# Transposing the weights piece by piece inside the forward chain, and storing them in on-chip layout, in a recurrent attention + SwiGLU training step

## The chip, the cores and the metric

One core of a Trainium2 chip. The metric is the device time of one execution in microseconds (us), lower is better. Before the prediction three executions of the kernel before were known: 3452.7 us median (3452.23 to 3463.88). A difference counts as faster or slower when it is over 2%. DRAM below is the device memory outside the core, SBUF the on-chip memory.

## The reference, cut to what matters

A forward pass and all its gradients. A sequence of 2048 tokens of width 448 goes through layer norm and an attention with memory in 64 *serial* segments: each takes 8 memory rows from the one before it. A SwiGLU feed-forward network (FFN) follows. The outputs are the result and nine gradients.

```python
# S=2048, D=448, H=16, Dh=256, M=8, seg=32 -> 64 segments;  FFN width F=1792; all bf16
for s in range(n_seg):
    h = concat([mem, x[s*32:(s+1)*32]])          # 40 rows
    q, k, v = h @ Wq, h @ Wk, h @ Wv             # 448 x 4096 each
    o = softmax(mask(q @ k.T * scale)) @ v
    o = o @ Wo                                   # 4096 x 448
    mem = o[:8]; outs.append(o[8:])
...
h  = x + attention(layernorm(x), mem0, Wq, Wk, Wv, Wo)
h2 = h + (silu(n @ w_gate) * (n @ w_up)) @ w_down,  n = layernorm(h)
out, vjp = jax.vjp(f, x, mem0, Wq, Wk, Wv, Wo, w_gate, w_up, w_down)
return (out, *vjp(grad_out))
```

## The kernel before

There are four stages, one after the other: the forward chain (64 segments), the FFN with its backward pass (8 groups of 2 tiles of 128 tokens), the backward chain (64 segments in reverse), and the weight gradients ("last stage"). The forward chain uses the weights as they lie. The FFN's backward pass and the backward chain need them *transposed*, and the kernel makes these transposes by DMA at the moment when a stage starts.

`W`, `A` and `B` are three large SBUF arenas; the numbers are offsets in KB per partition. In the profile `arW`, `arA` and `arB` are these arenas, so "arA<-arA" is a transpose inside SBUF.

```python
def transposed_rows(k, dst, src2d, tmp):                # removed by the change
    for kc in range(3):
        nc.sync.dma_start_transpose(out=dst[:, kc, :], in_=src2d[:, kc * P:(kc + 1) * P])
    nc.sync.dma_start_transpose(out=tmp, in_=src2d[:, k.D - P:k.D])
    nc.sync.dma_start(out=dst[0:64, 3, :], in_=tmp[64:P, :])
...
# forward chain, once per tile (4 segments): turn a block in SBUF, then store it
    def to_token_major(blk, t):
        for hf in range(2):
            ot = stg()                                  # one of two 8 KB staging buffers
            nc.sync.dma_start_transpose(out=ot..., in_=blk[:, 16 * hf:16 * hf + 16, :]...)
            nc.gpsimd.dma_start(out=dr["X_o"][t][:, hf * 2048:(hf + 1) * 2048], in_=ot)
...
# FFN: 48 transposes of 448 KB for the last stage (z, u, g of 16 tiles)
    def tmajor(src, t, tt, dst):
        stg = tstg_b[rot[0] % 3]
        nc.sync.dma_start_transpose(out=stg, in_=src[:, tt]...)
        nc.gpsimd.dma_start(out=dst[t * P:(t + 1) * P, :], in_=stg...)

    for gi in range(NT // G):
        for tt in range(G):
            nc.sync.dma_start(out=h_t, in_=dr["Hh"][rows, :])
            nc.vector.tensor_scalar(out=hn_t[:, 0:D], in0=h_t, ...)           # layer norm
            nc.sync.dma_start_transpose(out=hnT[...], in_=hn_t)
            nc.sync.dma_start(out=dout_t[:, 0:D], in_=GO2[rows, :])
            nc.sync.dma_start_transpose(out=doT[...], in_=dout_t)
        if gi == 0:
            transposed_rows(k, WdT_sb, Wd2, wdT_tmp)                          # w_down^T
            nc.gpsimd.dma_start(out=Wd_sb, in_=Wd2...)
            nc.sync.dma_start_transpose(out=WgT_sb, in_=Wg2)                  # w_gate^T
            nc.sync.dma_start_transpose(out=WuT_sb, in_=Wu2)                  # w_up^T
        ...
            dh_t = k.f32("f3", D, "dh_t")                                     # one buffer
            ln_bwd(k, [(dh_t[:], ...)], ...)
            nc.gpsimd.dma_start(out=dr["DH"][rows, :], in_=dh_t[:])
...
# backward chain, before its first segment
    transposed_rows(k, WoT_sb, k.Wo2, woT_tmp)
    prep_tile(NT - 1)
    load_seg(NSEG - 1)          # transposing loads of VG, QT, KT; plain load of P_all
    for (Wsrc, WT) in ((k.Wk2, WkT_sb), (k.Wv2, WvT_sb), (k.Wq2, WqT_sb)):
        nc.sync.dma_start_transpose(out=WT, in_=Wsrc)
...
# last stage: 96 transposing loads of 512 KB (X_v, X_k, X_q), and packed loads of M_v, M_k, M_q
            nc.sync.dma_start_transpose(out=x_t.rearrange(...), in_=dr["X_" + nm][t][:, ...])
            nc.gpsimd.dma_start(out=ld, in_=dr["M_" + nm][...]...)
```

## Time and profile before

| stage (from, to; us) | length | DMA share | granted TensorE clock |
|---|---|---|---|
| forward chain, 150 to 1160 (inside it) | 1010 | 0.44 | 0.99 |
| forward's last matmul (1181.3) to the start of the second backward segment's softmax gradient (1659.4) | 478.1 | 0.93 | 0.83 |
| backward chain, 1660 to 2730 (inside it) | 1070 | 0.79 | 0.98 |
| last stage, 2734.5 to 3461.7 | 727.2 | 0.72 | 0.98 |

The second row, "between the chains", holds the whole FFN and both of its borders. Its lines and the others come from the busy table by stretches of the kernel before. The columns are: stretch, its length, then busy time (and number of instructions) of TensorE, of TensorE's weight load, of VectorE, ScalarE and GpSimd, the granted clock, the mean busy share of the 16 DMA engines, and GB/s. The DMA share adds up the time that packets took. It can pass 1, and it does not measure bytes.

```profile
150.00:1160.00 1010.00, 950.83 (x23283) 736.94 (x23281) 428.97 (x978) 319.23 (x700) 151.75 (x351) 0.99 0.44 140
1181.30:1659.40 478.10, 312.87 (x2565) 220.53 (x2564) 240.77 (x373) 117.32 (x208) 79.13 (x147) 0.83 0.93 196
2734.50:3461.70 727.20, 682.80 (x3928) 316.70 (x3930) 88.15 (x157) 96.09 (x148) 124.21 (x216) 0.98 0.72 184
```

TensorE is busy 94% of the forward chain and of the last stage, and 65% of the stretch between the chains (312.87 of 478.1). The next lines are TensorE's timeline in that stretch (start, length, engine and line, output<-inputs, count; in brackets the idle time just before and what ended it).

```profile
1243.36 13.43 PE L536 MATMUL psf<-arA,arW 128*128 128x256 bf16 x96 [62.03 <-DMA arA<-arA]
1610.84 4.60 PE L713 MATMUL psf<-arA,arW 128*128 128x40 bf16 x128 [44.81 <-POOL arA L648]
1643.58 7.11 PE L756 MATMUL po<-arW,arA 128*32 128x448 bf16 x96 [19.58 <-DMA arW<-in_A_Wv_dram]
```

There are three holes: 62 us between the forward chain and the first FFN matmul, 45 and 20 us around the first backward segment. The chain of waits of the kernel before (start, length, what) shows who fills them: the sync queue (SPq), which issues weight transposes one after another.

```profile
1181.68 19.15 SPq L241
...
1211.56 16.71 SPq L556
...
1581.71 18.37 SPq L682
...
1628.03 15.50 DMA arW<-in_A_Wv_dram
```

L241 is `transposed_rows` on w_down, L556 the transpose of w_gate, L682 one attention weight. Last, TensorE's waits summed from 1181 to 1653 (engine and line <- releaser: total us, times, longest):

```profile
PE psf L536 <- DMA arA<-arA: 68.7, 6, 62.0
PE psf L713 <- POOL arA L648: 44.8, 1, 44.8
PE psf L536 <- DVE arA L565: 20.5, 6, 5.8
PE po L756 <- DMA arW<-in_A_Wv_dram: 19.6, 1, 19.6
```

The third line is the FFN's gate multiply, held by the one `dh_t` buffer. Some 126 us of TensorE idle time lie in the three holes.

### The profile page before, as it was taken

Reading aid. Unit: us, or ns where it says so; the run is one execution under the profiler, and the core shown is the slowest. Engines: PE = TensorE matmul, PEld = TensorE weight load, DVE = VectorE, ACT = ScalarE, POOL = GpSimd, SP = SyncE. Lnnn points to the kernel's source line nnn. Section 1 sums busy time; section 2 is a strip of 40 time slices with the busy share of each in tenths; the row PEclk is TensorE's granted clock in tenths of the full one; section 3 lists DMA queues with packets and bytes.
Section 4 is the critical chain, followed back from the end, with each engine's and each line's share of the span. In section 5 each row is a group of like instructions: output and inputs, shape, how many; then the busy total and the mean of one; then the engine's idle time right before and its main releaser. Section 6 shows DMA issues by size and latency. Waiting matters only on the chain.

```text
span 3461.7 us, 120955 instructions
## 1 busy us (share of the span) xinstructions
PE 3042.7 (88%) x55028; PEld 2056.9 (59%) x55038; DVE 1321.4 (38%) x2921; ACT 974.9 (28%) x2181; POOL 620.8 (18%) x1304
## 2 busy tenths in 40 slices
PE   3999999999999658892999999989999898999999
PEld 2777777777777446661666666666666544444444
DVE  4444444444444246771444444444444301111111
ACT  1333333333333223330333333333333202111100
POOL 3111111111111111111112211211221211111121
PEclk8999999999999879996999999999999999999999
DMA  7344633543534797799687878787887988888661
GB/s 264 132 130 133 174 127 130 162 146 127 156 130 147 134 210 182 178 212 239 139 164 167 174 161 165 166 160 163 172 167 162 275 241 185 174 176 179 160 247 38
DMA packets 997173, 583.91 MB, mean 169 GB/s; under 512 B 906100, under 2 KB 916420, under 8 KB 995060
## 3 DMA queue, kind: packets, MB, share of 16 engines
q1 hardware_dynamic: 926788, 340.27, 47.5%
q0 software_dynamic: 67568, 233.95, 19.8%
q8 instruction: 430, 7.05, 0.9%
q10 hardware_dynamic: 2304, 1.97, 0.2%
q14 instruction: 83, 0.68, 0.1%
HBM read 104.05 MB, written 250.19 MB: 102 GB/s over the span
## 4 chain that ended last, share of the span: by engine, by line
PE 61%; issue 13%; DMA 9%; DVE 8%; SPq 4%; ACT 2%; POOL 2%; ACTq 0%; DVEq 0%; POOLq 0%
PE psf L360 12%; PE po L756 8%; PE psf L399 6%; PE psf L713 5%; PE psf L691 4%; PE po L437 3%; PE fx L462 3%; PE fx L815 3%; PE psf L536 2%; PE psf L921 2%; PE psf L942 2%; PE psf L778 2%; DVE arA L75 2%; PE psf L446 2%; PE fx L602 2%
## 5 line engine op out<-in xcount | busy, mean ns | idle before, releaser
L77 ACT CAST arA<-psf 128x320 bf16<-128x320 f32 (+4 forms) x1139 | 487.9, 447 | 1595.2 <-PE psf L360 422.0
L75 DVE CAST arA<-psf 128x384 bf16<-128x384 f32 (+6 forms) x1029 | 492.5, 496 | 1075.9 <-PE psf L921 359.9
L360 PE MATMUL psf<-arA,arW 128*128 128x40 bf16 x16384 | 433.6, 181 | 62.0 <-POOL arA L345 35.8
L360 PEld LDWEIGHTS <-arW 128*128 128x128 bf16 x16384 | 432.2, 97 | 76.5 <-issue 57.3
L756 PE MATMUL po<-arW,arA 128*32 128x448 bf16 x6144 | 359.2, 365 | 40.5 <-DVE arA L75 21.0
L713 PE MATMUL psf<-arA,arW 128*128 128x40 bf16 x8192 | 219.2, 180 | 55.5 <-POOL arA L648 44.8
L921 PE MATMUL psf<-arW,arA 128*128 128x512 bf16 x990 | 250.7, 381 | 10.3 <-DMA arW<-X_k 5.3
L713 PEld LDWEIGHTS <-arW 128*128 128x128 bf16 x8192 | 214.9, 96 | 75.2 <-issue 74.8
L399 PE MATMUL psf<-arW,arA 128*64 128x512 bf16 x2048 | 259.5, 382 | 0.0
L756 PEld LDWEIGHTS <-arA 128*32 128x32 bf16 x6144 | 156.3, 98 | 160.7 <-issue 32.9
L536 PE MATMUL psf<-arA,arW 128*128 128x256 bf16 x1344 | 163.8, 283 | 94.4 <-DMA arA<-arA 68.7
L921 PEld LDWEIGHTS <-arA 128*128 128x128 bf16 x1440 | 135.2, 98 | 184.7 <-issue 39.2
L536 PEld LDWEIGHTS <-arW 128*128 128x128 bf16 x1344 | 136.3, 102 | 124.3 <-issue 100.4
L399 PEld LDWEIGHTS <-arA 128*64 128x64 bf16 x2048 | 147.3, 111 | 66.5 <-issue 0.2
L75 DVE CAST arB<-psf 40x320 bf16<-40x320 f32 x320 | 108.0, 337 | 98.1 <-PE psf L428 64.7
L77 ACT CAST arB<-psf 128x96 bf16<-128x96 f32 (+1 forms) x320 | 98.3, 307 | 103.5 <-DVE arB L75 51.0
L691 PEld LDWEIGHTS <-arW 128*128 128x128 bf16 x2048 | 88.4, 101 | 65.7 <-issue 62.1
L723 ACT COPY arA<-psf 128x1024 bf16<-128x1024 bf16 x128 | 123.3, 1015 | 4.7 <-PE psf L722 3.1
L462 PE MATMUL fx<-arW,arA 128*128 128x448 bf16 x512 | 124.5, 353 | 0.0
L437 PE MATMUL po<-arW,arB 128*8 128x448 bf16 x2048 | 110.7, 359 | 3.7
L691 PE MATMUL psf<-arB,arW 128*128 128x80 bf16 x2048 | 99.1, 203 | 16.7 <-DVE arB L740 7.7
L942 PE MATMUL psf<-arW 128*128 128x448 bf16 x450 | 95.4, 361 | 5.4 <-DMA arW<-X_o 5.3
(461 smaller groups left out, 3760.6 us busy)
## 6 DMA issues: line engine op xcount, KB each, us to landing
QT<-arA POOLq DMA_DIRECT2D x64, 512.0 KB, 4.0
KT<-arA SPq DMA_DIRECT2D x64, 512.0 KB, 3.5
VG<-arA SPq DMA_DIRECT2D x64, 512.0 KB, 3.1
X_o<-arA POOLq DMA_DIRECT2D x40, 512.0 KB, 4.5
X_v<-arA POOLq DMA_DIRECT2D x32, 512.0 KB, 6.2
X_k<-arA POOLq DMA_DIRECT2D x32, 512.0 KB, 4.2
X_q<-arA POOLq DMA_DIRECT2D x32, 512.0 KB, 4.2
arW<-X_o SPq DMA_DIRECT2D x30, 512.0 KB, 13.9
```

Source lines behind the costliest of these rows:

```text
L75: nc.vector.tensor_copy(out=out, in_=in_)
L77: nc.scalar.copy(out=out, in_=in_)
L360: nc.tensor.matmul(pss[b][:, jj * L:(jj + 1) * L], lhsT=W_sb[:, kc, c * P:(c + 1) * P], rhs=hT_roll[:, kc, sl, :], start=(kc == 0), stop=( ...
L399: nc.tensor.matmul(pV[b][64 * g:64 * g + 64, 0:512], lhsT=hT_flat[:, kc, sl * L:sl * L + 64], rhs=Wv_sb[:, kc, n * 512:(n + 1) * 512], sta ...
L437: nc.tensor.matmul(pO[32 * (j % 4):32 * (j % 4) + M, 0:D], lhsT=o8[:, j, :], rhs=Wo_sb[:, cj(j), :], start=(j < 4), stop=(j >= MC - 4), sk ...
L462: nc.tensor.matmul(px[:, 0:D], lhsT=xblk[:, j, :], rhs=Wo_sb[:, cj(j), :], start=(j == 0), stop=(j == MC - 1))
L536: nc.tensor.matmul(ps[:, f2 * 256:(f2 + 1) * 256], lhsT=Wt[:, kc, c * P:(c + 1) * P], rhs=xT[:, kc, :], start=(kc == 0), stop=(kc == KC - 1))
L691: nc.tensor.matmul(ps[b][:, i * 2 * L:(i + 1) * 2 * L], lhsT=lhs[:, cl, :], rhs=rhs_bd[:, cl // 2, :, :].rearrange("p g n -> p (g n)"), st ...
L713: nc.tensor.matmul(pss[b][:, jj * L:(jj + 1) * L], lhsT=WoT_sb[:, kc, c * P:(c + 1) * P], rhs=do_roll[:, kc, sl, :], start=(kc == 0), stop ...
L756: nc.tensor.matmul(pH[32 * (j % 4):32 * (j % 4) + 32, 0:D], lhsT=blk[nm][:, j, r * SEG:(r + 1) * SEG], rhs=WT[:, cj(j), :], start=(nm == " ...
L921: nc.tensor.matmul(pa[2 * kc + g][:, 0:w], lhsT=lhs_of(b)[:, kc * P:(kc + 1) * P], rhs=rhs_of(b, g), start=(b == 0), stop=(b == nblk - 1), ...
L942: nc.tensor.matmul(pa[i][:, 0:D], lhsT=lhs_of(b, i), rhs=rhs_of(b), start=(bi == 0), stop=(bi == len(nblk) - 1))
```

## The change

Intent: make the transposes early, where the DMA engines are half idle (share 0.44 in the forward chain), write them to DRAM in the layout that SBUF needs, and load them later with plain, large DMAs. FFN buffers move over regions that the forward chain frees early, so that the first FFN operands can load during the last segment. The first FFN operands are transposed by TensorE instead of by DMA. `dh_t` gets a second buffer. The last two FFN groups swap places.

```diff
+    for nm in ("q", "k", "v"):
+        dr["T" + nm] = dt("T" + nm, [P, MC, D])          # new DRAM tensors, 19.3 MB in all
+    dr["To"] = dt("To", [P, KC, HD]); dr["Td"] = ...; dr["Tg"], dr["Tu"] = ...
 ...
+    def piece():                                          # 44 pieces of 512 rows or columns
+        nm, Ws, i0, n = pieces.pop(0)
+        T, ot = dr["T" + nm], stg()
+        if nm in "do":
+            nc.sync.dma_start_transpose(out=o4[:, 0:3, 0:n], in_=Ws[i0:i0 + n, 0:3 * P])
+            nc.sync.dma_start_transpose(out=o4[:, 3, 0:n], in_=Ws[i0:i0 + n, D - P:D])
+            nc.gpsimd.dma_start(out=T[:, 0:3, i0:i0 + n], in_=o4[:, 0:3, 0:n])
+            nc.gpsimd.dma_start(out=T[0:64, 3, i0:i0 + n], in_=o4[64:P, 3, 0:n])
+        else:
+            nc.sync.dma_start_transpose(out=o3, in_=Ws[:, i0:i0 + n])
+            nc.gpsimd.dma_start(out=T[:, i0 // P:i0 // P + m, :], in_=o3)
     for s in range(NSEG):
 ...
+        if r < 3 and s >= 4:                              # three segments of every four
+            piece()
 ...
-            transposed_rows(k, WdT_sb, Wd2, wdT_tmp)
-            nc.sync.dma_start_transpose(out=WgT_sb, in_=Wg2)
-            nc.sync.dma_start_transpose(out=WuT_sb, in_=Wu2)
+    nc.gpsimd.dma_start(out=WdT_sb[:, 0:3, :], in_=dr["Td"][:, 0:3, :])     # during the last segment
+    nc.gpsimd.dma_start(out=Wd_sb, in_=Wd2...)
+    nc.gpsimd.dma_start(out=WgT_sb, in_=dr["Tg"])
+    nc.gpsimd.dma_start(out=WuT_sb, in_=dr["Tu"])
 ...
-    for gi in range(NT // G):
+    for n, gi in enumerate(list(range(last - 1)) + [last, last - 1]):
+                if n == 0:
+                    nc.tensor.transpose(pt[...], src[...], k.ident[:, :])   # 16 of these
+                else:
+                    nc.sync.dma_start_transpose(out=dst[...], in_=src)
+        if n == last:
+            nc.gpsimd.dma_start(out=wot[...], in_=dr["To"]...)              # inside the last group
+            nc.gpsimd.dma_start(out=W(64, k.MC, D), in_=dr["Tv"])
-            dh_t = k.f32("f3", D, "dh_t")
+            dh_t = k.f32(("f3", "f1")[tt], (D, DP)[tt], "dh_t")[:, 0:D]
 ...
-    transposed_rows(k, WoT_sb, k.Wo2, woT_tmp)
-    for (Wsrc, WT) in ((k.Wk2, WkT_sb), (k.Wv2, WvT_sb), (k.Wq2, WqT_sb)):
-        nc.sync.dma_start_transpose(out=WT, in_=Wsrc)
+    nc.gpsimd.dma_start(out=WkT_sb, in_=dr["Tk"])
+    nc.gpsimd.dma_start(out=WqT_sb, in_=dr["Tq"])
 # cut: the new buffer offsets, memsets, the square root in two parts, the order of issue
```

The code of the backward chain's loop and of the last stage is not touched.

## The prediction

> What bounds the kernel now. Four stages, as the busy table by 50 us stretches shows: forward chain (to 1181 us), FFN (1243 to 1566), backward chain (to about 2730), weight gradients. TensorE is busy 88% of the span and bounds each stage. Between stages it stops. TensorE's timeline shows it idle for 62 us from 1181.3 (ended by a DMA landing in the normalised-input tile), 44.8 us from 1566.0 and, after 13 us of the first backward segment, 19.6 us until transposed Wv has landed. That segment ends at 1652.7; later ones take about 16 us. In these holes the 16 DMA engines are full (share above 1.1 in the stretches table), and the chain of waits runs through the sync queue: 19.2 us of w_down transposes, 16.7 us for w_gate, 18.4 us for one attention weight. All weight transposes (19.5 MB) are made there, ahead of the small transposes that the matmuls wait for.
>
> What the change does. 44 pieces of the transposes go into the forward chain, three per tile, and back to DRAM; later they are plain loads. FFN buffers lie in regions freed earlier, so its first inputs and w_gate load during the last segment; its first operands are turned by 16 matmuls (under 2 us). Wo^T and Wv^T load inside the last FFN group, Wk^T and Wq^T after it. dh_t gets a second buffer, and the last two FFN groups swap, so the last tile's gradient is ready early.
>
> Estimates:
> - Forward to FFN: the hole shrinks from 62 to 2-8 us: the first gate matmul needs only loads begun 15 us before. Gain about 57.
> - FFN: 289 us of matmul in 323 us. DVE's 19.5 us wait for the store of dh_t, and the 20.5 us that TensorE waits for the gate multiply behind it, partly go. Gain about 10, net of stalls in the first group, whose weights land one after another.
> - FFN to backward: the first segment's Wo work moves inside the FFN tail. Its probabilities load sits behind the Wk^T load on the GpSimd queue, which waits for the last stores. A 3.6 MB load takes 6-10 us (the four initial weight loads end 6 to 11 us apart), so the first segment should end 35-40 us after the FFN's last matmul, instead of 87, with some 20 us of idle left. Gain about 45 after the moved work.
> - Forward chain: DMA share rises from 0.45 to about 0.65. Buffers are double and a segment takes 17.5 us, so pieces mostly fit; delayed K and Q stores and two activation-table reloads cost 0-15 us, say 6. [...] the forward stage has room (0.45), the boundary had none.
>
> Predicted: 3452.7 - 57 - 10 - 45 + 6, rounded to 3348 us, range 3322 to 3382. Chances: faster by over 2% 0.91, within 2% 0.08, slower 0.01.
>
> Right if: a TensorE hole under 10 us where 62 were; about 20 us idle in the first backward segment, ended by the GpSimd copy of the probabilities or by Wk^T or Wq^T landing; forward ending within 10 us of 1181; its DMA share near 0.65; no gate multiply waiting behind dh_t stores.
>
> Wrong if: pieces take over 8 us each, so that three in one segment delay the K store beyond its two-segment slack; the serial GpSimd queue, which holds the FFN loads behind stores that wait for transposes, starves the first FFN group (10 to 25 us); contention stretches the last two weight loads; transposes rather than dh_t limit the FFN.

## The result, and the profile after

| | median us | range | executions |
|---|---|---|---|
| before | 3454.09 | 3452.23 to 3463.88 | 4 |
| after | 3451.43 | 3449.1 to 3465.13 | 4 |

Executions over 1.5% slower than the fastest of the same kernel are left out of the means. A ratio is the mean time of one kernel's runs over that of the other's runs of the same rounds, so it is not quite the ratio of the medians. Here it is 0.9999, with a 95% interval of 0.9976 to 1.0023: the same time. Some 105 us were expected and nothing came. Both kernels were profiled at a mean granted clock of 0.957 and 0.958.

The busy table by stretches, kernel after, with the same stages (forward; between the chains; last stage):

```profile
150.00:1160.00 1010.00, 940.16 (x22833) 728.81 (x22834) 419.28 (x957) 315.81 (x690) 179.66 (x398) 0.98 0.62 177
1208.80:1619.10 410.30, 314.30 (x2580) 219.40 (x2577) 239.10 (x372) 119.60 (x211) 84.77 (x163) 0.88 0.93 218
2685.70:3447.30 761.60, 699.25 (x3928) 321.67 (x3930) 88.20 (x157) 96.09 (x148) 123.68 (x216) 0.95 0.73 176
```

To see what repeats, both kernels were run and profiled once more, unchanged (runs b_again and a_again below). This ledger cuts each of the four traces at the same instructions; lengths in us.

| part | before | b_again | after | a_again | difference of the means | predicted |
|---|---|---|---|---|---|---|
| start to the last forward matmul | 1181.3 | 1186.7 | 1208.8 | 1218.8 | **+29.8** | +6 |
| hole, forward to first FFN matmul | 62.0 | 48.2 | 2.9 | 3.9 | **-51.7** | -57 |
| first to last FFN matmul | 322.7 | 325.5 | 366.4 | 377.9 | **+48.1** | -10 |
| last FFN matmul to second backward segment | 93.4 | 89.5 | 41.0 | 41.4 | **-50.3** | -45 |
| backward chain | 1075.1 | 1066.6 | 1066.6 | 1062.4 | -6.4 | 0 |
| last stage | 727.2 | 735.5 | 761.6 | 767.1 | **+33.0** | 0 |

By this cut the two holes closed almost exactly as predicted. But the FFN got 48 us longer, the forward chain 30 us, and the last stage, whose code and instruction order are the same in both kernels, 33 us. TensorE's timeline of the kernel after shows what the FFN now contains:

```profile
1211.70 12.39 PE L575 MATMUL psf<-arW 128*128 128x256 bf16 x112 [0.84 <-DVE arW L75]
1227.76 0.82 PE L575 MATMUL psf<-arW 128*128 128x256 bf16 x3 [3.67 <-DMA arW<-Td]
1237.02 1.23 PE L575 MATMUL psf<-arW 128*128 128x256 bf16 x5 [8.44 <-DMA arW<-Td]
1250.18 0.53 PE L637 MATMUL fx<-arW,arA 128*128 128x448 bf16 x1 [9.40 <-DMA arW<-in_B_w_down_dram]
...
1568.32 1.05 PE L783 MATMUL psf<-arA 128*64 128x40 bf16 x32 [25.24 <-DMA arA<-VG]
1569.30 8.76 PE L656 MATMUL fx<-arW,arA 128*128 128x448 bf16 x40
1598.48 1.22 PE L743 MATMUL psf<-arB,arA 128*128 128x80 bf16 x16 [20.42 <-POOL arB L710]
```

The first group starves for 21.5 us while its weights land one after another. At the end, after the first matmuls of the backward chain, TensorE waits 25 us for one transposing load of VG, which took 28.4 us to land where the median is 5.2 (of the 32 of 64 whose landing the profile tells). This is a wait of the backward chain, but it falls before the last FFN matmuls (L656) in TensorE's order, so the ledger counts it in the FFN. After its last matmuls (L656) it waits 20 us for GpSimd's copy of the probabilities. The waits of the kernel after, from 1210 to 1612, say the same in sum. The gate multiply of before (20.5 us) is gone:

```profile
PE psf L783 <- DMA arA<-VG: 25.2, 1, 25.2
PE psf L743 <- POOL arB L710: 20.4, 1, 20.4
PE psf L575 <- DMA arW<-arW: 13.6, 4, 6.3
PE psf L575 <- DMA arW<-Td: 12.1, 2, 8.4
PE fx L637 <- DMA arW<-in_B_w_down_dram: 9.4, 1, 9.4
```

**Between the chains.** The DMA share over the whole stretch is 0.93 in both kernels. As packet time, averaged over the 16 engines, this is 0.93 x 478.1 = 445 us before and 0.93 x 410.3 = 382 us after: 63 us less packet time, 68 us less time. The stretch shrank by about as much as the packet time, not by the 112 us that its three terms (57, 10 and 45) had promised. The table of DMA queues of the same stretch (queue, kind: packets, MB, share of the 16 engines) shows the two queues that matter; q1 carries the sync queue's transfers, q0 GpSimd's (over the whole span of before, GpSimd's issues add up to 233.9 MB and q0 to 233.95). Before, then after:

```profile
q1 hardware_dynamic: 209361, 56.04, 68.1%
q0 software_dynamic: 8674, 37.40, 24.6%
```

```profile
q1 hardware_dynamic: 125289, 33.23, 52.1%
q0 software_dynamic: 9587, 55.61, 40.2%
```

Times the length of the stretch, q1 fell from 326 to 214 us of packet time, and q0 rose from 118 to 165. The transposes left, but the weights still have to come in, and that costs 47 us of the 112 that were saved.

**The forward chain.** The waits of TensorE from 150 to 1160, kernel before and then kernel after, changed notably in one kind only, called "issue": idle time for which the profile shows no releaser.

```profile
PE psf L360 <- issue: 6.9, 12, 1.2
PE psf L391 <- issue: 2.4, 5, 0.6
```

```profile
PE psf L356 <- issue: 11.2, 17, 1.2
PE psf L412 <- issue: 8.8, 12, 1.6
```

9.3 us became 20.0 (and 24.4 in a_again). The mean matmul of this stretch also takes 41.18 ns instead of 40.84 (busy time over count, lines above), at a clock of 0.98 instead of 0.99; over about 23,900 matmuls that is 8 us. Together these give most of the 22 to 28 us by which the stretch from the 3rd to the 63rd softmax grew. Another 6 us come in the last segment, where VectorE waits for a load that the normalised FFN input needs, ahead of work for the chain.

**The last stage.** Its 3928 matmuls are busy 699 us instead of 683, at a clock of 0.95 instead of 0.98, and they wait longer. First before, then after; this is TensorE's timeline in the gradient of Wk:

```profile
3055.45 1.24 PE L921 MATMUL psf<-arW,arA 128*128 128x512 bf16 x5 [1.06 <-DMA arW<-X_k]
...
3057.79 1.24 PE L921 MATMUL psf<-arW,arA 128*128 128x512 bf16 x5 [0.88 <-DMA arW<-X_k]
```

```profile
3019.49 2.29 PE L973 MATMUL psf<-arW,arA 128*128 128x512 bf16 x5 [3.71 <-DMA arW<-X_k]
...
3023.14 2.29 PE L973 MATMUL psf<-arW,arA 128*128 128x512 bf16 x5 [0.94 <-DMA arW<-X_k]
```

The same five matmuls take 2.29 us after a wait of 3.71 us, and again after the next wait of 0.94 us: 1.85 times as long as the 1.24 us before, where the waits are of about 1 us only. The granted clock goes with it: it stands at 0.50 from 3018.65 us, 2.9 us into the longer wait, for 10.24 us, over both groups of matmuls; before, it is 1.00 from 3055 to 3060 us. What makes the clock fall was not tested. In these two profiles TensorE had been idle for more than half of the 3.41 us (the shortest stretch at half clock here) before every fall in this stage, with up to 1.64 us of matmuls in them. In all, counting the stretches that lie wholly inside the last stage, the clock stood at half for 58.0 us in both profiles of after, for 17.1 and 23.9 us in those of before. So a load that was late cost twice here: 3.71 us as a wait, and 1.05 us more for each five matmuls at half clock. Why the loads are late in unchanged code is what most of the experiments are about. The landing times of the 96 transposing loads of this stage (minimum, median, maximum), as far as the profile tells them (59 of them before, 48 after):

```profile
DMA to landing us min/median/max: 4.5/5.3/13.7
```

```profile
DMA to landing us min/median/max: 4.7/5.7/11.2
```

### The profile page after: what moved, and what is told of

Its sections match the earlier page's. It is cut to its first block, busy times and chain, and to the rows that moved or that the text cites. A ratio compares the mean times of both kernels' runs of the same rounds, so it can differ in the third digit from the quotient of the medians.

```text
span 3447.3 us, 121182 instructions
## 1 busy us (share of the span) xinstructions
PE 3065.8 (89%) x55044; PEld 2066.5 (60%) x55054; DVE 1320.1 (38%) x2924; ACT 978.0 (28%) x2186; POOL 655.2 (19%) x1369
## 3 DMA queue, kind: packets, MB, share of 16 engines
q8 instruction: 430, 7.05, 0.9%
## 4 chain that ended last, share of the span: by engine, by line
PE 64%; DMA 11%; issue 10%; DVE 9%; ACT 2%; SPq 2%; POOL 1%; ACTq 0%; DVEq 0%; POOLq 0%
PE psf L356 12%; PE po L808 7%; PE psf L420 6%; PE psf L765 5%; PE psf L973 5%; PE psf L743 4%; PE po L458 3%; PE psf L994 3%; PE fx L485 3%; PE fx L867 3%; PE psf L830 2%; DVE arA L75 2%; PE psf L467 2%; DVE arB L75 1%; SPq L938 1%
## 5 line engine op out<-in xcount | busy, mean ns | idle before, releaser
L973 PE MATMUL psf<-arW,arA 128*128 128x512 bf16 x990 | 258.8, 390 | 17.3 <-DMA arW<-X_k 8.8
L765 PEld LDWEIGHTS <-arW 128*128 128x128 bf16 x8192 | 215.5, 97 | 34.8 <-issue 29.4
L575 PE MATMUL psf<-arW 128*128 128x256 bf16 x1344 | 157.5, 277 | 33.2 <-DMA arW<-arW 13.6
L1022 POOL DMA_DIRECT2D out_dram<-arA x96 | 51.8, 547 | 278.7 <-DVE arA L75 271.3
```

What stands on the lines that cost most here:

```text
L575: nc.tensor.matmul(ps[:, f2 * 256:(f2 + 1) * 256], lhsT=Wt[:, kc, c * P:(c + 1) * P], rhs=xT[:, kc, :], start=(kc == 0), stop=(kc == KC - 1))
L765: nc.tensor.matmul(pss[b][:, jj * L:(jj + 1) * L], lhsT=WoT_sb[:, kc, c * P:(c + 1) * P], rhs=do_roll[:, kc, sl, :], start=(kc == 0), stop ...
L973: nc.tensor.matmul(pa[2 * kc + g][:, 0:w], lhsT=lhs_of(b)[:, kc * P:(kc + 1) * P], rhs=rhs_of(b, g), start=(b == 0), stop=(b == nblk - 1), ...
```

## The experiments

Sixteen kernels ran, in four calls, on the chips numbered 5, 9, 4 and 5; each call has its own runs of the kernel before. All ratios are to that kernel. All results were correct except in the one run that is wrong. In the tables, "last stage" and "between" (the chains) are from single profiles; "X landing" is the median landing time of the last stage's transposing loads (of those whose landing the profile tells).

The build places DRAM tensors in the order of their first use. The new T tensors are first used in the forward chain, so everything first used later lies 19.3 MB further up. The build's own addresses say: X_v moved from 156.578 MB to 175.891 MB, and the other tensors of the last stage by the same distance. "Offset" below is the fraction of a MB in these addresses (0.578 before, 0.891 after); it is also that of X_k and X_q.

### Call 1: what repeats, the pieces alone, the addresses alone

b_again and a_again are the two kernels, unchanged.

> The kernel before, unchanged, to get a second profile of it. In the first pair of profiles the weight-gradient stage (from the last backward segment's softmax product to the end) took 727 us before and 762 us after the change, although its instruction order is identical in both. If that is scatter between executions, this stage may come out anywhere from 725 to 765 us here and the total from 3452 to 3464. If it is a real effect of the change, it should be 727 us again, within 5. Forward chain's last softmax at 1168 us, within 3.

> The changed kernel, unchanged, to get a second profile. Scatter theory: the weight-gradient stage comes out different from the 762 us of the first profile, by more than 10 us. Real effect: 762 within 5 again. Forward chain's last softmax at 1189 us, within 3, FFN start hole and the two holes at the start of the backward chain (25 and 20 us) as before; total 3447 to 3465 us.

Measured: 0.9994 (0.9948 to 1.0041) and 1.0000 (0.9967 to 1.0034). The null result stands, and the ledger above shows that the parts repeat within some 15 us: the difference of a single part from a single profile is no evidence below that. Several of the narrow bounds set here were missed: the last stage came out 8 us (b_again) and 5 us (a_again) longer than in the first profiles, and the last softmax of the forward chain 5 and 10 us later.

b_pieces is the kernel before with the 44 pieces in the forward chain, their results unused:

```diff
+    (the T tensors and piece(), as in the change)
+        if r < 3 and s >= 4:
+            piece()
```

> The kernel before, with the 44 transposed pieces of the weights made in the forward chain and stored to DRAM exactly as in the change, and nothing made of them (FFN and backward chain turn the weights themselves as before). Contention theory: the forward chain's last softmax moves from 1168 to about 1188 us, the holes around the FFN stay (62, 45, 20 us), total about 20 us above before (3475). Rival, that the forward chain lost its 21 us to the reordered FFN inputs at its end and to the two activation-table reloads: the forward chain stays within 5 us of 1168 and total within 5 us of before. If placement of the DRAM buffers slows the weight-gradient stage, 30 us come on top (about 3505).

b_shift does not make the pieces, it only touches each T tensor with one 128-byte store, so that the later tensors lie where the changed kernel has them:

```diff
+        T = dr["T" + nm]
+        if i0 == 0:
+            nc.gpsimd.dma_start(out=T[0:1, 0, 0:64], in_=ident[0:1, 0:64])
```

> The kernel before, with the seven new DRAM tensors declared and touched by one 128-byte store each: the DRAM addresses of the stored gradients that the last stage reads are then those of the changed kernel (19.3 MB higher), without the pieces' traffic. Placement theory: the weight-gradient stage goes from 727 to about 760 us, total about 3485. Rival, that placement does not matter: stage and total as in the kernel before of the same chip, within 5 us.

| run | ratio (95%) | forward, 3rd to 63rd softmax | last stage | X landing |
|---|---|---|---|---|
| before (from the first comparison) | 1 | 1038.9 | 727.2 | 5.3 |
| b_pieces | 1.0220 (1.0184 to 1.0256) | 1066.9 | 777.6 | 6.0 |
| b_shift | 1.0123 (1.0083 to 1.0162) | 1040.3 | 775.3 | 6.0 |

Moving addresses, with no other work to speak of, costs 1.2%, and in the profile nearly all of it lies in the last stage: busy 699 us at clock 0.95, as in the changed kernel. The forward chain of b_shift is that of before. So there are two losses, and the pieces carry both. Both kernels cost more than had been expected (3537.7 us for b_pieces where about 3505 stood, 3505.7 for b_shift where 3485 stood).

```profile
2735.50:3510.80 775.30, 699.09 (x3938) 323.10 (x3930) 88.16 (x157) 96.09 (x148) 123.84 (x216) 0.95 0.73 175
```

### Call 2: the addresses put back, and two repairs of the border

a_placed is the changed kernel with fourteen tiny stores in the third segment, one to each later tensor, before the first piece. They fix the order of first use, so these tensors get the addresses they had before the change and the T tensors come behind them. b_pieces_placed is b_pieces with the same stores.

```diff
+        if s == 2:
+            for nm in ("X_o", "Hh", "HN", "Zt", "DU", "DGP", "DH", "DHb", "X_v", "M_q", "M_v", "M_k", "X_k", "X_q"):
+                (a store of two elements to the start of dr[nm])
```

> The changed kernel with 14 four-byte touches of the older DRAM tensors in segment 2, so that the allocator gives the stored gradients X and M exactly the addresses that they have in the kernel before (156.6 to 216.6 MB) and puts the new tensors behind them. Placement theory, by the address of X: the weight-gradient stage falls from 762-767 us to 727-736 us, total 3420 to 3430 us, ratio 0.988 to before. Rival, that the size of the whole DRAM area or anything else of the change slows that stage: it stays at 760 or more and the total at 3455 to 3460.

> The kernel before with the pieces in the forward chain (results unused), X and M at their addresses of before. If the 75 us of the pieces at the shifted addresses are two separate costs, this is about 30 us above before (3490), all in the forward chain between its 3rd and 63rd softmax (about 1065 us against 1039-1043); weight-gradient stage 727 to 736. If the pieces themselves slow the last stage, that stays near 775 and the total near 3535.

a_fixA is a_placed with the FFN's weight loads on the sync queue, ahead of the last segment's small transposes, and the first normalised input issued after the chain's work on VectorE:

```diff
-    nc.gpsimd.dma_start(out=WdT_sb[:, 0:3, :], in_=dr["Td"][:, 0:3, :])
+    nc.sync.dma_start(out=WdT_sb[:, 0:3, :], in_=dr["Td"][:, 0:3, :])
 (the same for Wd, WgT, WuT)
+    with tc.issue_after(wu.ins):
+        k.last_rows()                 # the last tile's to_token_major, moved here
+            k.last_p = k.last_ev      # hn of the first group waits for the last P^T eviction
```

> The changed kernel with old addresses, and the FFN's start edited: w_down^T, w_down, w_gate^T, w_up^T loads on the sync queue ahead of the last token-major transposes (which come after them), and the first normalised inputs after, not before, the last segment's eviction of the transposed probabilities. Theory, that the first group starved because its loads sat on the GpSimd queue behind stores that wait for those transposes: the three holes of the first group (3.7, 8.4, 9.4 us) and the 5 us stop in the last forward segment vanish, total 20 to 27 us below the old-address version. Rival: the loads are limited by the DMA engines, and the holes stay at over 12 us in sum.

a_fixB is a_placed with the load of Wv^T issued behind the transposing load of VG, on the same queue, and with two buffers moved so that the last segment's probabilities can load earlier:

```diff
-        if n == last:
-            nc.gpsimd.dma_start(out=W(64, k.MC, D), in_=dr["Tv"])
+    vg = load_seg(NSEG - 1)
+    with tc.issue_after(vg.ins):
+        nc.sync.dma_start(out=WvT_sb, in_=dr["Tv"])
-    tstg_b = [W(92, FC, P), W(120.5, FC, P), B(4.75, FC, P)]
+    tstg_b = [W(92, FC, P), W(120.5, FC, P), B(5, FC, P)]
-    junk = B(3.75, D)
+    junk = B(8.5, D)
```

> The changed kernel with old addresses, and two edits at the FFN's end: the Wv^T load is issued on the sync queue behind the first segment's VG transpose instead of on the GpSimd queue ahead of it; and the probabilities of that segment lie clear of the FFN's buffers, so that their load does not wait behind the Wk^T load. Theory, that the two holes (25 us for the VG transpose beside the Wv^T load, 20 us for the probabilities) are these orders: the VG transpose lands in under 8 us instead of 28, no hole of 20 us waits for the GpSimd copy, and the total is 25 to 40 us below the old-address version. Rival, that the DMA engines are simply full there (14.7 MB of attention weights in one place): the waits move to Wk^T and Wq^T, gain under 10 us.

| run | ratio (95%) | forward, 3rd to 63rd softmax | between | TensorE idle in it | last stage | X landing |
|---|---|---|---|---|---|---|
| a_placed | 0.9922 (0.9875 to 0.9969) | 1073.4 | (slow) | (slow) | 743.1 | 5.4 |
| b_pieces_placed | 1.0043 (1.0003 to 1.0083) | 1059.3 | 463.8 | 150.9 | 737.5 | 5.2 |
| a_fixA | 0.9866 (0.9826 to 0.9907) | 1067.1 | 405.5 | 88.0 | 739.6 | 5.2 |
| a_fixB | 0.9897 (0.9859 to 0.9934) | 1066.8 | 406.4 | 88.7 | 739.2 | 5.3 |
| after, for comparison | 0.9999 | 1060.8 | 410.3 | 95.9 | 761.6 | 5.7 |

Three things follow. With the old addresses the last stage is back near 740 us, and the change is faster by 0.8%, or 1.0 and 1.3% with a repair. The pieces alone now cost 0.4% instead of 2.2%; their cost in the forward chain is still there. And the two repairs of the border, each of which removes the wait it aims at, hardly shorten the stretch between the chains. a_fixA removed the 6 us at the end of the forward chain (from the 63rd softmax to the last matmul 27.6 us instead of 34.5 in after) and the starving first group, but the waits of TensorE for the DMA transposes of FFN inputs and for later loads grew in return. a_fixB cut the wait for VG from 25.2 to 6.2 us, but a wait of 16.7 us for KT stands in its place, and the one for w_down^T grew from 12.1 to 18.8 us. The profile of a_placed fell in the slow state (two of its six runs were slow), so its FFN is not used. How long TensorE waits for VG differs much between profiles of kernels without the second repair: 25.2 us in after, 30.8 in a_again, 10.8 in a_fixA and 11.4 in a_pad000 of call 4, all fast. a_pad000 has no repair at all and took 404.2 us between the chains, so a stretch of 404 to 406 us is no evidence for a repair.

The last-stage line of a_placed answers to the three shown above: 686 us busy at clock 0.98.

```profile
2756.10:3499.20 743.10, 685.77 (x3938) 317.81 (x3930) 88.13 (x157) 96.09 (x148) 123.87 (x216) 0.98 0.70 181
```

### Call 3: height or alignment, transposes or stores, both repairs

b_pad16 and b_pad03 are the kernel before with one unused DRAM tensor in front. The first is 16 MB: everything lies higher by nearly as much as the change moved it, but the offset stays 0.578. The second is 0.3125 MB: hardly higher, but with the changed kernel's offset, 0.891.

```diff
+    pad = dt("PAD", [16384, 512])          # b_pad16;  [320, 512] in b_pad03
+    nc.gpsimd.dma_start(out=pad[0:1, 0:64], in_=ident[0:1, 0:64])
```

> The kernel before with one unused DRAM tensor of exactly 16 MB ahead of all its others (touched by one 128-byte store), so that every DRAM buffer lies 16 MB higher at the same offset within a megabyte (X at 0.578). If the slower last stage of the shifted buffers comes from how high they lie, that stage takes about 770 us here and the ratio to before is near 1.012. If it comes from their alignment (offset 0.578 against 0.891 MB), the stage takes 727 to 743 us and the ratio is within 0.5% of 1.

> As the last run, with 0.3125 MB instead of 16 MB: the offset within a megabyte becomes that of the changed kernel (0.891) and the height hardly changes. Alignment theory: last stage about 770 us, ratio near 1.012. Height theory: 727 to 743 us and ratio within 0.5% of 1.

b_turn_only is b_pieces_placed without the stores of the pieces to DRAM; only their transposes are left:

```diff
-            nc.gpsimd.dma_start(out=T[:, 0:3, i0:i0 + n], in_=o4[:, 0:3, 0:n])
-            nc.gpsimd.dma_start(out=T[0:64, 3, i0:i0 + n], in_=o4[64:P, 3, 0:n])
-            nc.gpsimd.dma_start(out=T[:, i0 // P:i0 // P + m, :], in_=o3)
```

> The kernel before with the pieces transposed in the forward chain but not stored to DRAM (old addresses). The forward chain between its 3rd and 63rd softmax took 1039 to 1043 us without pieces and 1059 to 1073 with them. If the transposes are the cost (they take most of the added DMA time), it stays at 1055 to 1068 here. If the stores, or the GpSimd queue that waits to issue them, are the cost, it falls to under 1048.

a_fixAB has both repairs.

> The changed kernel with old addresses and both order edits (FFN start and FFN end). If the two gains are separate (0.9897 and 0.9866 against 0.9922 for old addresses alone, though with wide intervals), the ratio to before is 0.980 to 0.985, some 3405 us. If they are the same slack, it stays at 0.987.

| run | ratio (95%) | forward, 3rd to 63rd softmax | last stage | X landing |
|---|---|---|---|---|
| b_pad16 (offset 0.578) | 1.0015 (0.9969 to 1.0061) | 1043.1 | 757.3 | 5.4 |
| b_pad03 (offset 0.891) | 1.0108 (1.0059 to 1.0158) | 1041.2 | 754.0 | 6.1 |
| b_turn_only (offset 0.578) | 1.0070 (1.0022 to 1.0118) | 1062.1 | 752.8 | 5.5 |
| a_fixAB (offset 0.578) | 0.9887 (0.9841 to 0.9934) | 1067.6 | 748.8 | 5.3 |

The total times say alignment, not height: 16 MB cost nothing, 0.3 MB cost 1.1%, nearly as much as b_shift's 19.3 MB. The two intervals just touch (1.0061 and 1.0059). The median landing times agree, 5.4 against 6.1 us. But one thing missed: on this chip the last stage of the single profiles does *not* separate the two (757 and 754), nor does the time at half clock in it (54.6 and 44.4 us). The three kernels at offset 0.578 have 749 to 757 in this call, above the 727 to 743 of that offset elsewhere, and b_pad03 lies below the 762 to 778 of its own. b_pad03's profile is that of its fastest run (3485.1 us; the others took 3503.1 to 3514.2). So a last stage read from one profile is a weak witness; the ratios, made of four runs each, carry this verdict.

b_turn_only gives the forward loss without any store: 1062.1, the same as with them (1059.3), against 1039 to 1043 without pieces. So the transposes, without the stores, bring the whole loss (and 0.12 of the 0.19 by which the DMA share there rises, 0.44 to 0.56 of 0.63). Its waits in the forward chain, from 150 to 1160, have the same "issue" growth as the changed kernel's:

```profile
PE psf L366 <- issue: 16.3, 23, 1.9
PE psf L419 <- issue: 6.6, 10, 1.4
```

What is TensorE waiting for in these holes? The queue q8, of the kind "instruction" on the page, moves 7.05 MB in 430 packets of 16 KB. TensorE has 55,044 + 55,054 instructions in the kernel after; 7.05 MB over these is 64 bytes each. From these numbers I estimate that this queue carries TensorE's own program; no run shows it. Matching the packets' times with TensorE's holes in the forward chain gave this count of holes (over 0.1 us) that end 1.2 to 1.6 us after such a packet has landed:

| | before | b_again | b_pad16 | after | a_again | b_turn_only | b_pieces_placed |
|---|---|---|---|---|---|---|---|
| holes | 17 | 24 | 22 | 35 | 45 | 38 | 37 |
| us in them | 9.7 | 13.2 | 11.0 | 24.5 | 29.4 | 24.6 | 25.0 |
| DMA share there | 0.44 | 0.44 | 0.44 | 0.62 | 0.63 | 0.56 | 0.63 |

Most of these packets go without a hole: of some 180 in this stretch, 17 went with one before and 35 after. But the holes grow. About 14 us of extra holes (11 became 26 in the mean) line up with these packets in the profiles with the higher DMA share. If the packets' times are shifted by 0.5 to 6 us to either side, at most 16 holes of after still match, against 35; in before it is up to 15, against 17, so there the match alone says little. This is a match in time; no run changed this queue's transfers alone, so the cause is not isolated.

a_fixAB, with both repairs, is no better than one: 404.6 us between the chains, 83.4 of them idle on TensorE. Its waits in the FFN (1205 to 1560) have moved to the DMA transposes of the FFN inputs (arW<-arW):

```profile
PE psf L591 <- DMA arW<-arW: 31.5, 7, 12.1
PE psf L800 <- DMA arA<-VG: 10.3, 1, 10.3
PE psf L782 <- DMA arW<-To: 5.1, 1, 5.1
```

### Call 4: other offsets in the changed kernel, and the FFN without its transposes

a_pad578, a_pad000 and a_pad250 are the changed kernel with nothing but an unused tensor in front, which puts X_v at 176.578, 176.000 and 176.250 MB.

```diff
+    pad = dt("PAD", [704, 512])            # a_pad578; smaller in the other two
+    nc.gpsimd.dma_start(out=pad[0:1, 0:64], in_=ident[0:1, 0:64])
```

> The changed kernel with nothing added but one unused DRAM tensor of 0.6875 MB ahead of the others: X goes from 175.891 to 176.578 MB, the offset within a megabyte of the kernel before. Alignment theory: the transposing loads of the last stage land in 5.2 to 5.5 us at the median instead of 5.6 to 5.7, ratio to before 0.988 to 0.994. Rival (position among the other tensors matters): 5.6 or more, ratio 0.997 to 1.003.

> As the last run with 0.109 MB: X at whole megabytes (176.000). No theory predicts it; if only 0.891 is slow, 5.2 to 5.5 us and a ratio near 0.99; if 0.578 is the lucky one, 5.6 us or more and a ratio near 1.0.

> As the last run with 0.359 MB: X at an offset of 0.250 MB. Same two readings as for whole megabytes.

a_noturn is a_fixAB with the 48 DMA transposes of the FFN (`tmajor`) left out; their sources are stored unturned. Three weight gradients are wrong. It takes 48 transposes off the DMA engines and off the sync queue, and leaves TensorE's work alone.

```diff
     def tmajor(src, t, tt, dst):
-        nc.sync.dma_start_transpose(out=stg, in_=src[:, tt]...)
-        nc.gpsimd.dma_start(out=dst[t * P:(t + 1) * P, :], in_=stg...)
+        nc.gpsimd.dma_start(out=dst[t * P:(t + 1) * P, :], in_=src[:, tt]...)
```

> Wrong results on purpose: the old-address version with both order edits, and the 48 token-major transposes of the FFN left out (its buffers are stored as they lie, same bytes). Theory, that the DMA engines with these transposes hold the FFN between the chains: TensorE's idle time from the end of the forward chain to the second backward segment falls from 83 us to under 50, DMA share in the FFN well below 0.9, total 30 to 60 us below that version (about 3385). Rival, that queue order or dependencies hold it: idle stays above 70 and the total within 15 us.

| run | ratio (95%) | last stage | X landing | between | TensorE idle in it |
|---|---|---|---|---|---|
| a_pad578 | 0.9860 (0.9818 to 0.9902), two runs of four | 740.9 | 5.4 | (slow) | |
| a_pad000 | 0.9981 (0.9936 to 1.0027) | 764.4 | 5.7 | 404.2 | 88.9 |
| a_pad250 | 0.9961 (0.9907 to 1.0016) | 764.7 | 5.5 | (slow) | |
| a_noturn | 0.9741 (0.9715 to 0.9767) | 741.4 | 5.1 | 357.1 | 48.6 |

Of the four offsets tried in the changed kernel (0, 0.25, 0.578, 0.891), only 0.578 is clear of the kernel before. For 0.25 this is not settled: its interval overlaps that of a_placed, and its profile and that of a_pad578 fell in the slow state, so their last stages are a hint only. One line that reserves 0.69 MB gave 0.9860 where the change alone had 0.9999. That the T tensors still lie in front in a_pad578, and behind in a_placed, speaks against their order as the cause.

a_noturn shows what holds the stretch between the chains. Its line in the busy table:

```profile
1204.00:1561.10 357.10, 308.39 (x2580) 216.98 (x2581) 239.40 (x372) 119.97 (x211) 80.43 (x147) 0.93 0.64 193
```

The same TensorE work (2580 matmuls) now takes 357 us instead of 404.6, with the DMA share down from 0.93 to 0.64. In the unrepaired and the repaired versions the stretch took 404 to 410 us at 0.93 (423.2 us at 0.92 in a_again): moving waits about hardly shortened it, and taking the 48 transposes away did. So these 48 transposes cost it some 47 us. Whether they do so through the DMA engines or through the sync queue is not separated, for the edit relieves both: the sync engine's DMA-issuing instructions, which run one after another, take 278 of the 404.6 us in a_fixAB and 104 of the 357.1 in a_noturn. The trace of a_fixAB speaks for the queue in its longest wait for an FFN input, 12.1 us: the transpose that ended it was issued only 7.6 us after TensorE had begun to wait, behind other work of the sync queue, and landed 4.5 us later. A run with the same DMA work on a freer queue would decide it; there is none.

The best correct versions are a_pad578 (0.9860, on two runs) and a_fixA (0.9866). Both are ahead of the kernel before, with intervals clear of 1, though by less than the 2% that counts as faster here.

## Why the prediction was wrong, point by point

The sum was 3452.7 - 57 - 10 - 45 + 6. By terms:

1. **"Forward to FFN: Gain about 57": right.** 55 us of hole (mean of two profiles) became 3.4: a gain of 52. The expected "TensorE hole under 10 us" is there: 2.9. The 16 transposing matmuls before it were busy for 1.26 us.
2. **"FFN to backward: Gain about 45": right by its own cut, 50 measured**, with the first segment ending 33 us after the FFN's last matmul (foreseen 35 to 40). The remaining idle of 20.4 us was ended by the GpSimd copy of the probabilities, as foreseen. But the cut flatters this term. The 25.2 us wait for VG belongs to the first backward segment and lies before the cut only because 40 of the FFN's matmuls come after it. Counted with the border, together with the 4.7 us wait for Wo^T and the 5.8 us of moved work, the border gained 17 us and the FFN lost 8 (profile of after). What failed in it is "A 3.6 MB load takes 6-10 us": the load of Wv^T took 24.1 us, and 29.2 in a_again. The four initial weight loads that it was estimated from end 10.8, 11.0 and 13.3 us apart in the profile of before.
3. **"FFN: Gain about 10": this step failed; it lost 48.** The overlap was wrong: the loads that had stood in the holes were to run beside the FFN's matmuls almost for nothing, and the matmuls waited for them instead. The part about `dh_t` came true (20.5 us gone). But TensorE's waits inside the FFN rose from 33 us (20.5 for the gate multiply and 13 small ones) to 72: 21.5 in the starving first group, 25.2 for VG, 13.6 for transposes, 4.7 for Wo^T and some small ones. The warning "starves the first FFN group (10 to 25 us)" stood among the risks and not in the sum. The deeper fault is the method: I costed the holes and took the room for granted. The FFN already had a DMA share of 0.84, and most of the loads that had stood in the holes were put there. A sum of the DMA packet time over the whole stretch could have been made from the profile of before alone. Its q1 line is 5.8 us of packet time per MB (326 / 56.04), its q0 line 3.1 (118 / 37.40). Taking 19.5 MB of transposes out and putting as many MB of loads in gives an estimate of 445 - 113 + 61 = 393 us, and at the share of 0.93 a stretch of 423 us: a gain of 55 us where I had 112. This estimate was made afterwards, and it takes for granted that the share stays at 0.93. Measured: 410 and 423, after 478 and 463. a_fixA, a_fixB and a_fixAB tested the rival reading, that the order of the loads is to blame: each removed its wait and the stretch stayed at 404 to 406. a_noturn took the 48 transposes away and shortened it to 357; as said there, it does not tell the DMA engines from the sync queue.
4. **"Forward chain: say 6": mis-sized; 30 measured.** The range given was 0 to 15. Its DMA share, predicted 0.65, was 0.62. But no wait for late K and Q stores or for table reloads grew (the two added reloads took 1.28 us each): transposes alone (b_turn_only) give about 20 us, half of it or more (13 us: 24.6 against 11.3 in the mean of the three profiles without pieces) in holes that line up with packets of the instruction queue. About 6 us are the last segment's VectorE order; a_fixA removed them.
5. **The last stage, and with it the addresses, had no term; +33 measured.** Not a single instruction of it changed. Seven new DRAM tensors moved its inputs, and at the new offset its loads land 0.3 to 0.8 us later in the median. Waits grow, and the clock stands at half for longer (58.0 us of the stage in both profiles, against 17.1 and 23.9). b_shift reproduces it without any of the change (1.0123), b_pad03 with 0.3 MB (1.0108), b_pad16 shows that 16 MB at the old offset do nothing (1.0015), and a_placed and a_pad578 take it away in the changed kernel.

That the result is so near to zero is chance: gains of 108 us and losses of 111 us happen to cancel. Measured, the terms add up: +30 - 52 + 48 - 50 - 6 + 33 = +3 us, against +2.7 us for the difference of the mean spans (3456.8 to 3459.5).

One more thing was not in the sum; among the risks stood only "contention stretches the last two weight loads". The transposing load of VG, on the sync queue, ran beside the 3.6 MB load of Wv^T, on the GpSimd queue, and took 28.4 us to land, where the median is 5.2. How long it takes there is not steady: 33.3 us in a_again and 14.7 in a_pad000, and 53.9 to 69.9 in the three profiles of the slow state. How the two queues share the DMA engines was not shown. The prediction counted on delays in the forward chain, which "has room", and not at the FFN's end, where the new loads went.

What stays open: why an offset of 0.578 MB is better than 0, 0.25 or 0.891, and whether the transposing loads or the packed loads of M (4.6 us median before, 5.5 after) feel it more, since the runs moved both together (TensorE's waits behind the M loads grew from 17.7 to 26.9 us, those for X from 12.1 to 17.5); why the last stages of call 3 were long at both offsets; and why VG and Wv^T together take so long. The slow state's longer stretch between the chains in the three profiles that fell in it is this same wait: TensorE waited 51.9 us (a_pad578), 63.1 (a_pad250) and 68.3 (a_placed) for VG, against 25.2 in after, and few bytes moved meanwhile (74 GB/s in the last 33 us of it in a_pad250).

## What to carry to other kernels

Where two stages meet, add up the DMA packet time over the whole stretch, loads that only move included, before counting TensorE's holes: here, at a share of 0.93, closed holes reopened elsewhere. A background transfer need not be free where its engines have room on average: here it cost 20 us at a share of about 0.6, half of it or more in waits of TensorE that line up with packets of an instruction queue that nobody had listed. And when a stage that was not touched changes its time, look at addresses: run the old kernel with the new memory layout, and the new kernel with the old one, before explaining anything else.
